# Attention and feed-forward kernel: one order of work at the turns of half batches, and a batch's scores for both halves in one stretch, partly in free PSUM columns

## The chip, the cores and the metric

The kernel runs on one core of a Trainium2 chip. The metric is the device time of one execution, in microseconds (us). An execution is timed as a whole; the profile's span is the part of it between the first and the last instruction that the profiler records. The core has five engines with a queue each: PE (matmuls, with weight loads shown apart as PEld), DVE (vector), ACT (activations and copies), POOL (a second, slower vector engine) and SP, which here issues all DMA transfers in order. SBUF is the on-chip memory, PSUM the accumulators that PE writes and DVE and ACT read.

## The reference

For each of 8 batches (576 tokens, 8 heads of 64): an attention over 32 memories per head, then a gated feed-forward layer of width 512 → 2048 → 512.

```python
a   = softmax(phi, axis=2)                    # over the 576 tokens
k_m = einsum('bhsm,bhsd->bhmd', a, k);  v_m = einsum('bhsm,bhsd->bhmd', a, v)
p   = softmax(q @ k_m.T / 8, axis=-1)         # 576 x 32 per head
x   = (p @ v_m) as (4608, 512)
h   = x @ w_in
out = (h * clip(h + 3, 0, 6) / 6) @ w_out
```

All is float32. Because `p` has 32 columns per head, the kernel folds `v_m` into `w_in` once per batch ("fold", `fo`/`vh`/`vl`: the matmuls of L428 and their two halves of a number, L439 and L448) and multiplies the probabilities by the folded weights.

## The kernel before, in words

Float32 products are made from halves of numbers: a value is cast to a rounded part (**high**) and a remainder (**low**), and three matmuls (high·high, high·low, low·high) make one product.

**Stages.** Batches 0 to 2 serve to convert the weights as well. From batch `FIRST` = 3 on runs the steady stage: batches 3 to 7, each of two halves (256 and 320 tokens; of the 320 the last 64 go into a separate "rest" product). A half has 8 `Unit`s of 256 columns of the hidden layer, a unit two steps; so a batch has 32 **steps**, 0 to 15 for half 0 and 16 to 31 for half 1. At step s, in the order in which it is written (and so queued on every engine; nothing reorders it):

- `gemm1` (PE, L716): six matmuls into a bank `ph`; `relu` (ACT, L722); `gate` (DVE, L735, and in half 1 L739 for the rest).
- On odd steps the unit's sums: `sum_first` (DVE L745), `sum_second` (POOL L749, 256 columns, and L750, 128). On even steps `high(1)` (ACT L756, 128x512) and `low(1)` (DVE L761, 128x512) of the unit just summed.
- The words of the tables `EVERY`, `STEADY`, `FOURTH` for this step: a string such as `6 xa.N.0` puts the attention piece `xa.N.0` of the next batch (N; C is this batch, M the one after next) at step 6.
- On odd steps `high(0)` (ACT L756, 128x384) and `low(0)` (DVE L761, 128x384).
- `half_step(s-3)`: the unit's share of the second matmul (`products`, PE L688). The scheme takes seven products for eight: part 0 (A11, M5, M2) is nine matmuls into banks m0 and m1, part 1 (A22, M6, M7, M1) is twelve into m2 and m3, nine of them with weights that a DMA brings (`stream`, issued by `fetch_streams`, L684).

So PE does 15 or 18 matmuls a step. At the **turn** of a half (its last unit, at steps 18 and, of the next batch, 2), the four banks leave: `leave_first` and `leave_second` read them (ACT L789 to L795, DVE L798, L799), `leave_third` makes two additions of 128x512 on POOL (L803, L804) and then issues the store (SP, L806).

**Resting batches.** In batches 4 and 6, between steps 2 and 3, PE runs 96 matmuls for the rest columns of two batches (`rest_stage`, `RestUnit`, L822 to L829); the words of steps 0 to 2 are played within it.

**The attention words** that matter here: `fetch` loads folded-weight inputs (L217, 512 KB, a ring of two buffers); `xa` subtracts the maximum from phi (DVE L309, 128x512, and L306, 64x128 twice), `xe` is its exponential (ACT L313); `mem` (PE L323), `nr`/`nk`, `tp`/`tk` make the memories; `sc` is the scores (PE L361, 32x256 or 32x320 tiles, into the one buffer `psc`), `ct` their transposition (DVE L377); `cm` the maxima (DVE L387), `cs` their subtraction (POOL L391), `ex` the exponential (ACT L394), `ds` and `dr` sums and reciprocals (DVE L387, L398, L399), `dm` the scaling (POOL L403), `bt` the transposition back, `bh` (ACT L412) and `bl` (POOL L417) the halves of the probabilities.

Of the kernel before, what the change touches and what calls it, by code (L numbers as in the profile page):

```python
# [27 lines left out]
NG = 2  # L28
# [86 lines left out]
def attention_ffn_kernel(ctx: ExitStack, tc: tile.TileContext, pn, pt, kv, kl, qt, w1, w2, out):  # L115
# [584 lines left out]
    class Unit:  # L700
# [62 lines left out]
        def products(self, part):  # L763
# [8 lines left out]
            def stream(x):  # L772
# [4 lines left out]
                (("A22", 2, 1, kept(1)), ("M6", 3, 1, part and stream(1)), ("M7", 3, 0, part and stream(2)),  # L777
# [8 lines left out]
        def leave_first(self):  # L786
# [24 lines left out]
    sums = {}  # L811
# [144 lines left out]
    with tc.manual_schedule():  # L956
# [32 lines left out]
        UNBOUND = ("tw", "ts", "th", "to2", "rp", "fs")  # L989
# [49 lines left out]
        for s in range(total_steps + LAG + 1):  # L1039
# [8 lines left out]
            if s < total_steps:  # L1048
# [76 lines left out]
```

## Time and profile before

| | |
|---|---|
| median of three executions | 705.54 us (703.06, 705.54, 1340.69) |
| profiled execution, span | 705.24 us, 703.2 us |
| PE busy, share of the span | 680.7 us, 97% |
| DVE, ACT, POOL busy | 532.1, 388.1, 333.0 us |
| mean granted clock of PE | 0.998 |
| DMA traffic | 162.86 MB, mean 232 GB/s |

The page also gives the chain of work that ended last: PE 47%, DVE 27%, DMA 9%, ACT 7%, POOL 3%. The profiled execution took 705.24 us, 2.0 us more than its span. In the rows further down, the first two numbers of a timeline row are the start and the length in us, x9 says that nine alike stand together, and a bracket tells how long the engine had been idle before and what released it. On POOL and DVE a length includes time in which an instruction that has been issued waits for the other.

### The profile page before, as it was taken

What the parts mean: (1) busy time and instruction counts of PE and PEld (TensorE: products, weight loads), DVE (VectorE), ACT (ScalarE), POOL (GpSimd) and SP (SyncE); (2) the same over time, 40 slices, a digit from 0 to 9 for tenths busy, and PEclk for the clock granted to TensorE, in tenths of its full rate; (3) what the DMA queues carried; (4) which work ended last, traced back from release to release, by engine and by line L of the source; (5) the groups of instructions that cost most, each with busy time, mean ns of one, the idle gap of its engine ahead of it and who ended that gap; (6) DMA issues with size and microseconds to landing.
All of it is one profiled execution on the core that took longest, in us unless ns stands there. A gap on an engine that the chain in (4) does not pass through costs nothing.

```text
span 703.2 us, 14752 instructions
## 1 busy us (share of the span) xinstructions
PE 680.7 (97%) x5622; PEld 577.2 (82%) x5622; DVE 532.1 (76%) x962; ACT 388.1 (55%) x786; POOL 333.0 (47%) x333
## 2 busy tenths in 40 slices
PE   8999999999999999999999999899999999999997
PEld 3456777878877787789889998799988999889997
DVE  4899987776466455566998869977898778987765
ACT  4677785554344455554655655555465555655543
POOL 2645330396564574632545435453457334554433
PEclk9999999999999999999999999999999999999999
DMA  9988573655671784899673877749675593736351
GB/s 353 421 328 314 181 270 125 225 178 178 270 260 47 277 291 132 302 375 343 221 260 118 265 273 271 275 166 332 216 262 191 155 323 114 270 118 219 121 180 47
DMA packets 66270, 162.86 MB, mean 232 GB/s; under 512 B 6808, under 2 KB 13976, under 8 KB 63640
## 3 DMA queue, kind: packets, MB, share of 16 engines
q1 hardware_dynamic: 66120, 161.86, 65.2%
q8 instruction: 44, 0.72, 0.4%
q14 instruction: 26, 0.21, 0.1%
q10 hardware_dynamic: 80, 0.07, 0.0%
HBM read 135.68 MB, written 26.22 MB: 230 GB/s over the span
## 4 chain that ended last, share of the span: by engine, by line
PE 47%; DVE 27%; DMA 9%; ACT 7%; issue 4%; POOL 3%; SPq 2%; ACTq 0%; POOLq 0%; DVEq 0%
PE acc L688 17%; PE acc L545 11%; PE ph L491 7%; PE ph L716 7%; DVE rounded L761 7%; DVE gated L735 3%; DVE gated L745 3%; DVE both L448 2%; DMA stream<-kept 2%; DMA w<-w_kept 2%; ACT rounded L756 2%; PE pk L323 2%; DMA kvt<-in_kv 2%; PE pv L428 2%; DMA kept<-stage 1%
## 5 line engine op out<-in xcount | busy, mean ns | idle before, releaser
L688 PE MATMUL acc<-w,rounded 128*128 128x256 f32 x1248 | 177.7, 282 | 4.4 <-DVE rounded L761 3.8
L688 PEld LDWEIGHTS acc<-w,rounded 128*128 128x128 f32 x1248 | 157.7, 188 | 26.7 <-issue 10.8
L749 POOL TENSOR_TENSOR gated<-gated 128x256 f32<-128x256 f32 x80 | 76.8, 961 | 189.0 <-DVE gated L735 158.2
L761 DVE TENSOR_TENSOR rounded<-gated,rounded 128x384 fp32r<-128x384 f32 (+1 forms) x160 | 133.2, 833 | 38.0 <-ACT rounded L756 32.5
L716 PE MATMUL ph<-probs,both 128*128 128x256 f32 (+1 forms) x960 | 150.4, 292 | 0.0
L756 ACT CAST rounded<-gated 128x384 fp32r<-128x384 f32 (+1 forms) x160 | 90.6, 567 | 95.3 <-DVE gated L745 89.2
L716 PEld LDWEIGHTS ph<-probs,both 128*128 128x128 f32 x960 | 131.6, 188 | 0.2
L722 ACT ACTIVATE gf<-ph,three 128x256 f32<-128x256 f32 (+1 forms) x160 | 79.9, 499 | 42.3 <-PE ph L716 40.7
L545 PE MATMUL acc<-w,ghi 128*128 128x512 f32 x384 | 101.0, 398 | 0.1
L688 PE MATMUL acc<-stream,rounded 128*128 128x256 f32 x720 | 97.3, 279 | 1.5 <-DMA stream<-kept 1.3
L688 PEld LDWEIGHTS acc<-stream,rounded 128*128 128x128 f32 x720 | 88.6, 188 | 3.6 <-DMA stream<-kept 2.5
L545 PEld LDWEIGHTS acc<-w,ghi 128*128 128x128 f32 x384 | 68.9, 188 | 23.9 <-issue 5.7
L735 DVE SCALAR_TENSOR_TENSOR gated<-gf,ph 128x256 f32<-128x256 f32 x160 | 65.5, 410 | 27.0 <-ACT gf L722 26.9
L491 PEld LDWEIGHTS ph<-probs,both 128*128 128x128 f32 x528 | 75.0, 188 | 11.2 <-DVE gf L507 5.2
L491 PE MATMUL ph<-probs,both 128*128 128x256 f32 (+1 forms) x528 | 78.5, 297 | 2.7 <-DVE gf L507 2.6
L507 DVE SCALAR_TENSOR_TENSOR gf<-gf,ph 128x576 f32<-128x576 f32 x44 | 33.0, 750 | 40.8 <-ACT gf L501 40.6
L501 ACT ACTIVATE gf<-ph,three 128x576 f32<-128x576 f32 (+2 forms) x52 | 36.5, 703 | 43.0 <-PE ph L491 38.1
L545 PE MATMUL acc<-w,glo 128*128 128x512 f32 x192 | 54.0, 390 | 0.0
L448 DVE TENSOR_TENSOR both<-pv,both 128x512 fp32r<-128x512 f32 x62 | 42.3, 682 | 14.9 <-ACT both L439 14.7
L525 DVE TENSOR_TENSOR glo<-gf,ghi 128x512 fp32r<-128x512 f32 x44 | 39.1, 892 | 12.8 <-PE acc L545 7.0
L439 ACT CAST both<-pv 128x512 fp32r<-128x512 f32 x62 | 36.1, 584 | 20.7 <-DVE both L448 13.6
L194 POOL TENSOR_TENSOR w<-tmp,raw 128x512 uint32<-128x512 uint32 x14 | 21.8, 1580 | 45.2 <-DVE tmp L184 24.5
(106 smaller groups left out, 886.9 us busy)
## 6 DMA issues: line engine op xcount, KB each, us to landing
stream<-kept SPq DMA_DIRECT2D x186, 256.0 KB, 4.4
kvt<-in_kv SPq DMA_DIRECT2D x32, 516.0 KB, 7.0
w<-w_kept SPq DMA_DIRECT2D x32, 512.0 KB, 6.0
raw<-in_w SPq DMA_DIRECT2D x16, 512.0 KB, 8.6
raw<-in_w SPq DMA_DIRECT2D x8, 1024.0 KB, 7.9
out_t<-o SPq DMA_DIRECT2D x16, 512.0 KB, 3.3
w<-w_kept SPq DMA_DIRECT2D x8, 1024.0 KB, 7.8
kept<-stage SPq DMA_DIRECT2D x24, 256.0 KB, 4.4
```

The costliest lines, as they stand in the source:

```text
L448: nc.vector.tensor_tensor(both[:, 1], src, both[:, 0].bitcast(F32), ALU.subtract)
L491: nc.tensor.matmul(dst, w[:, g, fs], x[:, g * n : (g + 1) * n], start=(i == 0), stop=(i == len(seq) - 1),)
L501: nc.scalar.activation(self.gf, self.h, AF.Relu, bias=three)
L525: nc.vector.tensor_tensor(self.glo[:, :n], self.gated(), self.ghi[:, :n].bitcast(F32), ALU.subtract)
L545: nc.tensor.matmul(accs[self.b, self.rest, k].rearrange("p (x c) -> p x c", c=VC), left[:, t * P : (t + 1) * P], w, start=k in self.first ...
L688: nc.tensor.matmul(dst, left[l], right[r], start=begin and n == 0, stop=end and n == 2, skip_group_check=True)
L716: nc.tensor.matmul(h, w[:, g, fs], x[:, g * self.n : (g + 1) * self.n], start=(i == 0), stop=(i == len(seq) - 1))
L722: nc.scalar.activation(self.gf, self.h[k], AF.Relu, bias=three)
L735: nc.vector.scalar_tensor_tensor(dst, by_tile(self.gf), 6.0, by_tile(self.h[k]), ALU.min, ALU.mult)
L749: nc.gpsimd.tensor_tensor(g[:, 2:4], g[:, 0::8], g[:, 1:8:6], ALU.subtract)
L756: nc.scalar.copy(self.parts[0][:, at], self.g[:, 1:8][:, at])
L761: nc.vector.tensor_tensor(low[:, at], self.g[:, 1:8][:, at], high[:, at].bitcast(F32), ALU.subtract)
```

## The change

1. The scores of both halves are made at step 14, behind that step's products (the word `later` divides the words of a step): half 0's into columns 256 to 511 of bank `ph0` and into the first 256 columns of the running half's bank m1, half 1's into `psc`; the transpositions follow (those of half 0 one per bank). Before, half 0's stood at step 16 and half 1's at step 20. The other attention words move with them, most to one step earlier.
2. The loads `fetch.N.0` and `fetch.N.1` move from steps 5 to 11 to steps 0 to 2, `fetch.N.3.1` from step 29 to 27; some of the words `vh`, `vl`, `bh.C.1`, `bl.C.1` move to one or two steps later.
3. In part 1 of the products M6 and M7 (bank m3) come first, then A22 and M1 (bank m2); `leave_second` reads m3 first.
4. `leave_third` becomes `leave_fourth`, `leave_fifth` and `store`: one addition behind the sums of each of the next two odd steps, the store behind that. In resting batches all three stay together at the first turn.

```diff
 STEADY = """
-0 fo.C.3 vh.C.3.0 vl.C.3.0 / 3 vh.C.3.1 / 4 vl.C.3.1 bh.C.1 / 5 bl.C.1
+0 fetch.N.0.0 fo.C.3 vh.C.3.0 / 1 fetch.N.0.1 vl.C.3.0 fetch.N.1.0 / 2 fetch.N.1.1 / 4 vh.C.3.1 / 5 vl.C.3.1 / 6 bh.C.1 / 7 bl.C.1
 """
 EVERY = """
-0 sp.N / 5 fetch.N.0.0 / 6 xa.N.0 / 7 xe.N.0 fetch.N.0.1 / 8 xa.N.1 xa.N.2 / 9 xe.N.1 fetch.N.1.0 / 10 xe.N.2 / 11 mem.N fetch.N.1.1
-/ 12 nr.N nk.N q.N.0 / 13 q.N.1 / 14 tp.N tk.N / 16 sc.N.0 ct.N.0 pt.M / 17 kv.M.0
-/ 20 sc.N.1 ct.N.1 pn.M / 21 cm.N.0 cs.N.0 cm.N.1 kv.M.1 / 22 fo.N.0 vh.N.0.0 vl.N.0.0 / 23 fetch.N.2.0 vh.N.0.1 vl.N.0.1 ex.N.0 cs.N.1 fetch.N.2.1
-/ 24 ds.N.0 dr.N.0 dm.N.0 mx.M.0 / 25 fo.N.1 vh.N.1.0 vl.N.1.0 ex.N.1 / 26 vh.N.1.1 vl.N.1.1 mx.M.1 fetch.N.3.0
-/ 27 ds.N.1 dr.N.1 bt.N.0 dm.N.1 mt.M mo.M kv.M.2 / 28 fo.N.2 vh.N.2.0 vl.N.2.0 bh.N.0 / 29 vh.N.2.1 vl.N.2.1 bl.N.0 fetch.N.3.1
-/ 30 bt.N.1 kv.M.3 / 31 kv.M.4
+0 sp.N / 5 xa.N.0 / 6 xe.N.0 / 7 xa.N.1 xa.N.2 / 8 xe.N.1 / 9 xe.N.2 / 10 mem.N
+/ 11 nr.N nk.N q.N.0 / 12 q.N.1 / 13 tp.N tk.N / 14 later sc.N.0 sc.N.1 ct.N.0 ct.N.1 / 15 pt.M / 16 cm.N.0 cs.N.0 pn.M / 17 kv.M.0
+/ 20 cm.N.1 cs.N.1 ex.N.0 kv.M.1 / 21 ds.N.0 dr.N.0 dm.N.0 / 22 fo.N.0 vh.N.0.0 vl.N.0.0 / 23 fetch.N.2.0 vh.N.0.1 vl.N.0.1 fetch.N.2.1
+/ 24 mx.M.0 ex.N.1 / 25 fo.N.1 vh.N.1.0 vl.N.1.0 bt.N.0 / 26 ds.N.1 vh.N.1.1 vl.N.1.1 fetch.N.3.0
+/ 27 dr.N.1 dm.N.1 mx.M.1 fetch.N.3.1 / 28 fo.N.2 vh.N.2.0 vl.N.2.0 bh.N.0 kv.M.2 / 29 mt.M vh.N.2.1 vl.N.2.1 bl.N.0 mo.M
+/ 30 kv.M.3 / 31 bt.N.1 kv.M.4
 """
...
+        def beside(self, hf):
+            return self.b > FIRST and hf == 0
...
+                if self.beside(hf):
+                    self.psc[hf] = [ph[0][:, W[0] :], sums[self.b - 1, 0][1][:, :VC]]
...
-                (("A22", 2, 1, kept(1)), ("M6", 3, 1, part and stream(1)), ("M7", 3, 0, part and stream(2)),
+                (("M6", 3, 1, part and stream(1)), ("M7", 3, 0, part and stream(2)), ("A22", 2, 1, kept(1)),
                  ("M1", 2, 0, part and stream(0))),
...
-            nc.vector.scalar_tensor_tensor(o[:, 0::3], m1, 1.0 / 6.0, x[:, 0::3], ALU.mult, ALU.subtract)
-            nc.vector.scalar_tensor_tensor(o[:, 0::3], m67, 1.0 / 6.0, o[:, 0::3], ALU.mult, ALU.add)
+            nc.vector.scalar_tensor_tensor(o[:, 0::3], m67, 1.0 / 6.0, x[:, 0:2], ALU.mult, ALU.subtract)
+            nc.vector.scalar_tensor_tensor(o[:, 0::3], m1, 1.0 / 6.0, o[:, 0::3], ALU.mult, ALU.add)
...
                 if k:
                     unit.sum_first()
                     unit.sum_second()
+                    if len(leaving) > 1:
+                        leaving.pop(0)()
...
+                for w in said[:soon]:
                         play(group(w))
...
             unit = half_step(s - LAG - 1, ...)
+            if s < total_steps:
+                for w in said[soon + 1 :]:
+                    play(group(w))
+            if not s % 2 and len(leaving) == 1:
+                leaving.pop()()
```

How the order of instructions moves at three places follows. In the changed kernel a line of the units has a number that is higher by 8 (L761 is now L769, L745 is L753, L749 and L750 are L757 and L758); of the attention by 2 to 8.

**First place: DVE at steps 5 to 8 of batches 4 to 7**, from the gate of step 5 on. `rounded<-gated` is a low part, `pnat<-pnat,nmxb` is `xa`, `both<-pv` is `vl.C.3.1`, `gated<-gated` is `sum_first`. Before:

```order
L735 SCALAR_TENSOR_TENSOR gated<-gf,ph_2966 128x256
L745 TENSOR_TENSOR gated<-gated 128x256
L761 TENSOR_TENSOR rounded<-gated,rounded 128x384
L735 SCALAR_TENSOR_TENSOR gated<-gf,ph_2965 128x256
L761 TENSOR_TENSOR rounded<-gated,rounded 128x512
L309 TENSOR_TENSOR pnat<-pnat,nmxb 128x512
L735 SCALAR_TENSOR_TENSOR gated<-gf,ph_2966 128x256
L745 TENSOR_TENSOR gated<-gated 128x256
L761 TENSOR_TENSOR rounded<-gated,rounded 128x384
L735 SCALAR_TENSOR_TENSOR gated<-gf,ph_2965 128x256
L761 TENSOR_TENSOR rounded<-gated,rounded 128x512
L309 TENSOR_TENSOR pnat<-pnat,nmxb 128x512
```

Now:

```order
L743 SCALAR_TENSOR_TENSOR gated<-gf,ph_2966 128x256
L753 TENSOR_TENSOR gated<-gated 128x256
L456 TENSOR_TENSOR both<-pv,both 128x512
L311 TENSOR_TENSOR pnat<-pnat,nmxb 128x512
L769 TENSOR_TENSOR rounded<-gated,rounded 128x384
L743 SCALAR_TENSOR_TENSOR gated<-gf,ph_2965 128x256
L769 TENSOR_TENSOR rounded<-gated,rounded 128x512
L743 SCALAR_TENSOR_TENSOR gated<-gf,ph_2966 128x256
L753 TENSOR_TENSOR gated<-gated 128x256
L311 TENSOR_TENSOR pnat<-pnat,nmxb 128x512
L308 TENSOR_TENSOR pnat<-pnat,nmxb 64x128 x2
L769 TENSOR_TENSOR rounded<-gated,rounded 128x384
```

`xa.N.0` (128x512) now stands between step 5's `sum_first` and its low part, and `xa.N.1`, `xa.N.2` between those of step 7; before, they stood behind the low parts of steps 6 and 8.

POOL at steps 5 and 7 (two sums each, and `bl.C.1` with `probs<-pT,probs`), before:

```order
L749 TENSOR_TENSOR gated<-gated 128x256
L750 TENSOR_TENSOR gated<-gated 128x128
L417 TENSOR_TENSOR probs<-pT,probs 128x640
L749 TENSOR_TENSOR gated<-gated 128x256
L750 TENSOR_TENSOR gated<-gated 128x128
```

and now:

```order
L757 TENSOR_TENSOR gated<-gated 128x256
L758 TENSOR_TENSOR gated<-gated 128x128
L757 TENSOR_TENSOR gated<-gated 128x256
L758 TENSOR_TENSOR gated<-gated 128x128
L425 TENSOR_TENSOR probs<-pT,probs 128x640
```

`bl.C.1` moves from behind step 5's sums to behind step 7's.

**Second place: POOL from the turn at step 18 on**, before (`o<-o` are the two additions, `st<-st,mx` is `cs`):

```order
L803 TENSOR_TENSOR o<-o 128x512
L804 TENSOR_TENSOR o<-o 128x2x256
L749 TENSOR_TENSOR gated<-gated 128x256
L750 TENSOR_TENSOR gated<-gated 128x128
L749 TENSOR_TENSOR gated<-gated 128x256
L750 TENSOR_TENSOR gated<-gated 128x128
L391 TENSOR_TENSOR st<-st,mx 128x512
```

and now, from step 19's sums on:

```order
L757 TENSOR_TENSOR gated<-gated 128x256
L758 TENSOR_TENSOR gated<-gated 128x128
L811 TENSOR_TENSOR o<-o 128x512
L399 TENSOR_TENSOR st<-st,mx 128x640
L757 TENSOR_TENSOR gated<-gated 128x256
L758 TENSOR_TENSOR gated<-gated 128x128
L815 TENSOR_TENSOR o<-o 128x2x256
L411 TENSOR_TENSOR st<-st,sm 128x512
```

Between the sums of steps 19 and 21 stand now one addition and `cs.N.1`, and behind those of step 21 the other addition and `dm.N.0`. DVE at steps 20 and 21 (gates, `sum_first`, `mx<-st` and `sm<-st` are reductions of `cm` and `ds`), before:

```order
L761 TENSOR_TENSOR rounded<-gated,rounded 128x512
L377 STREAM_TRANSPOSE st<-psc 128x640
L735 SCALAR_TENSOR_TENSOR gated<-gf,ph_2966 128x256
L739 SCALAR_TENSOR_TENSOR rest<-gf,ph_2966 128x64
L745 TENSOR_TENSOR gated<-gated 128x256
L387 TENSOR_REDUCE mx<-st 128x16
L387 TENSOR_REDUCE mx<-st 128x20
L761 TENSOR_TENSOR rounded<-gated,rounded 128x384
```

and now:

```order
L769 TENSOR_TENSOR rounded<-gated,rounded 128x512
L395 TENSOR_REDUCE mx<-st 128x20
L743 SCALAR_TENSOR_TENSOR gated<-gf,ph_2966 128x256
L747 SCALAR_TENSOR_TENSOR rest<-gf,ph_2966 128x64
L753 TENSOR_TENSOR gated<-gated 128x256
L395 TENSOR_REDUCE sm<-st 128x16
L406 TENSOR_SCALAR sm<-sm 128x16
L407 RECIPROCAL sm<-sm 128x16
L769 TENSOR_TENSOR rounded<-gated,rounded 128x384
```

The transposition of step 20 is gone from here, `cm.N.1` stands in its place, and step 21 has the sums and reciprocals of `ds.N.0`, `dr.N.0`.

**Third place: PE at the scores.** Before, step 16 (half 1's eight tiles stood the same way at step 20):

```order
L716 MATMUL ph_2965<-probs,both 128x320 x6
L361 MATMUL psc<-qh,kvT 32x256 x8
L688 MATMUL acc<-w_6_1556,rounded 128x256 x3
L688 MATMUL acc<-stream,rounded 128x256 x9
L716 MATMUL ph_2966<-probs,both 128x320 x6
```

and now, from the products of step 14 on:

```order
L696 MATMUL acc<-stream,rounded 128x256 x3
L368 MATMUL ph_2965<-qh,kvT 32x256
L368 MATMUL acc<-qh,kvT 32x256
L368 MATMUL ph_2965<-qh,kvT 32x256
L368 MATMUL acc<-qh,kvT 32x256
L368 MATMUL ph_2965<-qh,kvT 32x256
L368 MATMUL acc<-qh,kvT 32x256
L368 MATMUL ph_2965<-qh,kvT 32x256
L368 MATMUL acc<-qh,kvT 32x256
L368 MATMUL psc<-qh,kvT 32x320 x8
L724 MATMUL ph_2966<-probs,both 128x256 x6
L696 MATMUL acc<-w_6_1556,rounded 128x256 x9
```

Sixteen tiles stand together, those of half 0 in turn in `ph_2965` (bank `ph0`) and `acc` (bank m1); two blocks of matmuls (`gemm1` into `ph1` and nine products, of which the last three write m1) stand between them and the next `gemm1` into `ph0`.

## Rows read from the trace of the kernel before

**Rows 1.** Waits view, PE: engine, what, releaser: us in total, times, longest.

```profile
PE acc L688 <- DVE rounded L761: 3.8, 11, 0.4
```

**Rows 2.** Timeline of PE, batch 4, half 0: start, length, instruction, count, idle before.

```profile
391.36 0.84 PE L716 MATMUL ph<-probs,both 128*128 128x256 f32 x6
...
393.40 0.84 PE L716 MATMUL ph<-probs,both 128*128 128x256 f32 x6
...
397.82 1.55 PE L688 MATMUL acc<-w,rounded 128*128 128x256 f32 x9
```

**Rows 3.** Timeline of PE, batch 4, half 1: steps 16 and 20 with their scores.

```profile
413.23 1.03 PE L716 MATMUL ph<-probs,both 128*128 128x320 f32 x6
...
416.26 1.04 PE L716 MATMUL ph<-probs,both 128*128 128x320 f32 x6
...
422.29 1.03 PE L716 MATMUL ph<-probs,both 128*128 128x320 f32 x6
...
425.43 1.04 PE L716 MATMUL ph<-probs,both 128*128 128x320 f32 x6
```

**Rows 4.** Timeline of PE: waits for a low part and for loads.

```profile
446.51 0.39 PE L688 MATMUL acc<-w,rounded 128*128 128x256 f32 x2
447.19 1.09 PE L688 MATMUL acc<-w,rounded 128*128 128x256 f32 x7 [0.29 <-DVE rounded L761]
...
454.72 1.09 PE L428 MATMUL pv<-w,kvT 64*32 64x512 f32 x16 [1.64 <-DMA w<-w_kept]
...
535.68 1.87 PE L688 MATMUL acc<-stream,rounded 128*128 128x256 f32 x9 [0.58 <-DMA stream<-kept]
```

**Rows 5.** Timeline of DVE, batch 4, steps 4 to 8.

```profile
389.89 0.69 DVE L761 TENSOR_TENSOR rounded<-gated,rounded 128x512 fp32r<-128x512 f32 x1
...
393.69 1.71 DVE L761 TENSOR_TENSOR rounded<-gated,rounded 128x512 fp32r<-128x512 f32 x1
...
396.37 0.42 DVE L745 TENSOR_TENSOR gated<-gated 128x256 f32<-128x256 f32 x1
397.38 0.85 DVE L761 TENSOR_TENSOR rounded<-gated,rounded 128x384 fp32r<-128x384 f32 x1 [0.58 <-ACT rounded L756]
...
399.71 0.57 DVE L306 TENSOR_TENSOR pnat<-pnat,nmxb 64x128 f32<-64x128 f32 x2
```

**Rows 6.** Timeline of POOL, batch 4, steps 5 to 7.

```profile
392.55 0.46 POOL L750 TENSOR_TENSOR gated<-gated 128x128 f32<-128x128 f32 x1
392.97 1.89 POOL L417 TENSOR_TENSOR probs<-pT,probs 128x640 fp32r<-128x640 f32 x1
396.48 0.92 POOL L749 TENSOR_TENSOR gated<-gated 128x256 f32<-128x256 f32 x1 [1.63 <-DVE gated L735]
```

**Rows 7.** Timeline of ACT, batch 4, steps 6 and 7.

```profile
393.04 0.62 ACT L756 CAST rounded<-gated 128x512 fp32r<-128x512 f32 x1
394.34 0.48 ACT L722 ACTIVATE gf<-ph,three 128x256 f32<-128x256 f32 x1 [0.68 <-PE ph L716]
```

**Rows 8.** Timeline of DVE, the rest stage of batch 4.

```profile
378.64 1.37 DVE L829 TENSOR_TENSOR rounded<-total,rounded 128x128 fp32r<-128x128 f32 x1
```

**Rows 9.** Timeline of POOL, same place.

```profile
378.40 1.47 POOL L804 TENSOR_TENSOR o<-o 128x512 f32<-128x512 f32 x1
```

**Rows 10.** Timeline of DVE, batch 4, steps 20 and 21.

```profile
427.20 0.84 DVE L377 STREAM_TRANSPOSE st<-psc 128x640 f32<-128x640 f32 x1
...
428.73 1.40 DVE L387 TENSOR_REDUCE mx<-st 128x16 f32<-128x512 f32 x2
430.05 1.20 DVE L761 TENSOR_TENSOR rounded<-gated,rounded 128x384 fp32r<-128x384 f32 x1
```

**Rows 11.** Timeline of PE, batch 4, step 23: the products that read that low part.

```profile
431.67 1.18 PE L688 MATMUL acc<-w,rounded 128*128 128x256 f32 x9
```

**Rows 12.** Groups by form, POOL, whole span: busy us, mean ns, idle before.

```profile
L804 POOL TENSOR_TENSOR o<-o 128x512 f32<-128x512 f32 x10 | 13.4, 1339 | 1.7 <-DVE o L799 1.7
...
L391 POOL TENSOR_TENSOR st<-st,mx 128x640 f32<-128x640 f32 x8 | 12.5, 1565 | 2.0 <-DVE mx L387 2.0
```

More of the change, by code (lines that the diff above doesn't have):

```diff
@@ L250, in load_q @@
         loaded.setdefault(b, {})["q", hf] = heads
-    vw, probs = {}, {}
+    vw, probs, sums = {}, {}, {}
     class Attention:
@@ L349, in turned @@
             nc.scalar.copy(self.kvT, self.pq[:, :, :P])
+        def beside(self, hf):
+            return self.b > FIRST and hf == 0
         def scores(self, hf):
             if (self.b, hf) == (0, 1):
-                self.psc = [bank(W[hf]) for _ in range(NG)]
+                self.psc[hf] = [bank(W[hf]) for _ in range(NG)]
             else:
-                psc = self.psum("psc")
-                self.psc = [psc[:, g, : W[hf]] for g in range(NG)]
-                self.psc_whole = psc[:, :, : W[hf]]
+                if self.beside(hf):
+                    self.psc[hf] = [ph[0][:, W[0] :], sums[self.b - 1, 0][1][:, :VC]]
+                else:
+                    self.psc_whole[hf] = self.psum("psc")[:, :, : W[hf]]
+                    self.psc[hf] = [self.psc_whole[hf][:, g] for g in range(NG)]
             for j in range(NJ):
@@ L361, in scores @@
                     nc.tensor.matmul(
-                        self.psc[g][j * M : (j + 1) * M],
+                        self.psc[hf][g][j * M : (j + 1) * M],
                         self.kvT[rows, g, j * M : (j + 1) * M],
                         loaded[self.b]["q", hf][j][rows, :],
-                        start=True,
+                        start=not (self.beside(hf) and g),
                         stop=True,
                         tile_position=(g * D, j * M),
+                        skip_group_check=self.beside(hf),
                     )
@@ L372, in scores_turn @@
             st = st.rearrange("p (g s) -> p g s", g=NG)
-            if (self.b, hf) == (0, 1):
-                for g in range(NG):
-                    nc.vector.transpose(st[:, g], self.psc[g])
+            if (self.b, hf) == (0, 1) or self.beside(hf):
+                for g in (1, 0):
+                    nc.vector.transpose(st[:, g], self.psc[hf][g])
             else:
-                nc.vector.transpose(st, self.psc_whole)
+                nc.vector.transpose(st, self.psc_whole[hf])
         def by_token(self, hf):
@@ L809, in leave_third @@
             )
-    sums = {}
     class RestUnit:
@@ L987, in rows_of @@
             return {k: [w for w in ws if w.split(".")[0] in UNBOUND or int(w.split(".")[1]) < B] for k, ws in rows.items()}
-        UNBOUND = ("tw", "ts", "th", "to2", "rp", "fs")
+        UNBOUND = ("later", "tw", "ts", "th", "to2", "rp", "fs")
         n = starts[5]
@@ L1055, in attention_ffn_kernel @@
                     unit.sum_second()
+                    if len(leaving) > 1:
+                        leaving.pop(0)()
                 elif s >= 2 and not (resting and i == 2):
                     finish_unit(units[s // 2 - 1], 1)
+                said = rows.get(i, ())
+                soon = said.index("later") if "later" in said else len(said)
                 if not resting:
-                    for w in rows.get(i, ()):
+                    for w in said[:soon]:
                         play(group(w))
```

19 lines of the change are left out of this document (13 added, 6 removed).

## The prediction

> **What bounds the kernel now.** I read the page's share of busy time first: PE is busy 97% of the span, so what counts is whether PE gets longer work or waits. The waits view of PE then says for what it waits in the steady stage: eleven times for a low part from DVE, 3.8 us in all [rows 1], and the timeline has single waits for loads [rows 4]. Third comes the pace of PE: an even step of half 0 takes 393.40 − 391.36 = 2.04 us [rows 2], 18 matmuls at 0.113; in half 1 the six matmuls of L716 take 1.03 instead of 0.84 [rows 2, 3], so 2.04 + 0.19 = 2.23. Everything longer is an excursion or a wait. Last come DVE and POOL, for the low parts hang on them: a DVE instruction with two SBUF inputs stands still while POOL works. L761 with 512 columns, issued at 393.69, took 1.71 us, with POOL's L417 from 392.97 to 394.86 [rows 5, 6]: it ended 0.54 behind POOL's end. POOL also gets in between two DVE instructions that stand next to each other: its addition, issued at 378.40, ran ahead of DVE's small L829 of 378.64, which took 1.37 [rows 8, 9]. So what the change does to POOL's place in the order matters as much as what it does on PE.
>
> **The parts, against the profiled 705.24 us** (span 703.2 and 2.0 around it; the median of the runs shown, 705.54, is 0.3 above).
>
> *Waits for low parts that go.* An average wait shows 3.8/11 = 0.35 us of idle time [rows 1], but costs more: the nine matmuls from 446.51 on run to 448.28, so 1.77 instead of 1.18 [rows 4, 11], 0.59 where 0.29 is shown. With 0.29 or 0.30 on top that is 0.64 each. Eight of the eleven stand where the change moves the cause: three at step 29 (sums and transposition of step 27 now stand at 25 and 26), two at step 1, two at step 5 of the batches without a rest stage (two additions at once at the turn), one at step 21 of batch 7. About one of them returns, in halves, at steps 5 and 7, for the two additions still come there. 7 × 0.64 = **−4.5** (bounds 0 and 8 × 0.64 = −5.1).
>
> *Loads.* One `fo` waited 1.64 for its input [rows 4]; that load is issued two steps, some 4 us, earlier: **−1.64**. The products at 535.68 took 1.87 instead of 1.18 and had been idle 0.58 before [rows 4, 11]: 1.27, with a 512 KB load ahead of their streams that now goes earlier: **−1.27** (bound 0 each). The four loads put into steps 0 to 2 are 2 MB ahead of later streams on SP; in those steps no stream is due, so they cost nothing; if that cover is gone, one such wait a batch returns.
>
> *The joint excursion.* Step 16 took 416.26 − 413.23 = 3.03, so the scores of half 0 cost 0.80; step 20 took 3.14, so 0.91 [rows 3]. The 64 columns more cost 0.11, so 256 cost 0.44, and 0.36 is left that one excursion costs as such. Joined, it is paid once: −0.36. Against it stands that the scores must find step 14's `gate` done, since they write beside what it reads; they come 1.4 us behind `gemm1`, against relu and gate of the same step, and I put the wait at 0.3. Four batches have scores to make (4 to 7, in batches 3 to 6): 4 × −0.06 = **−0.2**. The trace has no such wait; the bounds are −0.91 each (all of one excursion) and +0.5.
>
> *Order of the products, slots, split of the additions as such*: as many instructions of the same shapes; 0. What the split moves is place 2.
>
> *Place 1: steps 5 to 9 of batches 4, 5 and 6* (batch 7 has no next batch, and in batch 3 other words stand there). `xa` now stands ahead of the low part instead of behind it. At step 5 it takes POOL's turn: L750 (0.46, at 392.55 [rows 6]) comes 0.5 later, so L756 starts at 393.5 instead of 393.04, and ACT has `bh` (640 columns, about 0.7) and the exponential of `xa.N.0` (512 columns, about the 0.62 of L756 [rows 7]) ahead of relu 7, which starts at 395.2 instead of 394.34 [rows 7]; `sum_first` of step 7 then starts at 396.1 (0.48 of relu [rows 7], and a gate of as many columns as L745 has, 0.42 [rows 5]), a little ahead of its 396.37 of now, because L309 no longer stands before it [rows 5]. From there DVE and POOL take turns: L749 (0.92 [rows 6]) to 397.2; L309 to 397.7 (POOL's end + 0.54, as above); L750 to 398.0; the first L306 to 398.2 (0.57 for two [rows 5]); `bl` on POOL, which took 1.89 with a wait of some 0.3 in it [rows 6], to 399.6; the second L306 to 399.8; and only now the low part, 0.45 more: 400.2. It ended at 397.38 + 0.85 = 398.23 [rows 5], and PE, which took 1.55 for these nine matmuls instead of 1.18 [rows 2, 11], was already waiting for it. So all of 400.2 − 398.2 ≈ 1.95 falls on PE: 3 × 1.95 = **+5.85** (bounds: 0, if `bl` comes behind the low part; 3 × 2.4, if every handover costs 0.15 more).
>
> *Place 2: steps 19 to 23 of batches 3 to 6.* POOL now has an addition behind step 19's sums, `cs.N.1` behind step 20, an addition behind step 21's sums. The first delays step 20's low part, but that has a margin: today L377 begins behind it at 427.20 [rows 10], and `cm.N.1`, about half of 1.40 [rows 10], takes the place of that 0.84, so DVE is free at about 427.9. Then `cs.N.1` runs on POOL, a mean of 1.57 [rows 12], some 1.3 without its own waits, to 429.2, and `sum_first` of step 21 ends 0.27 behind it (half of 0.54, for half the columns): 429.5. POOL's two sums end at 430.5 (0.92 + 0.46 [rows 6], less overlap), and the second addition (mean 1.34 [rows 12], 1.28 without waits) at 431.7. The low part of step 21, which stands behind the short `ds` and `dr`, ends 0.41 behind that (0.54 × 384/512): 432.15, instead of 430.05 + 1.20 = 431.25 [rows 10]. PE reads it with the third of the nine matmuls that begin at 431.67, at 431.90 [rows 11]; without step 20's excursion 0.91 earlier, at 430.99. The wait is 432.15 − 430.99 ≈ 1.2: 4 × 1.2 = **+4.8** (bounds 0, if the addition comes behind the low part, and 4 × 1.6, with the means of rows 12).
>
> The Trainium skill speaks against the shorter handovers used here: its page "SBUF — State Buffer", section "SBUF: two separate sides", calls the port pair of DVE and POOL an exclusive lock that is held for the whole instruction, while the other fully blocks. The blocking agrees with rows 5 and 6; the end at +0.54, where the same instruction takes 0.69 beside an idle POOL [rows 5], does not show a whole instruction behind POOL's end. By the page each of some three handovers at seven places would cost 0.15 more, an estimate of +3.2, and the sum would be about 711.5.
>
> *Sum.* −4.5 − 1.64 − 1.27 − 0.2 + 5.85 + 4.8 = +3.05, so 705.24 + 3.05 = **708.3 us**.
>
> **The rivals.** *A, as summed*: 708.3. *B, one of the two places does not bite* (DVE gets its low part in ahead of POOL): 708.3 − 5.85 = 702.4 or 708.3 − 4.8 = 703.5. For it: margins of 0.3 to 0.5 decide who is first at both. Against: POOL's instruction is queued ahead at each. *C, neither bites*: 705.24 − 7.6 = 697.6. Against it: DVE's 1.71 and 1.20 for low parts [rows 5, 10] show that one POOL instruction suffices. *D, the waits for low parts do not go but move on* (the change does not do what it says): 708.3 + 4.5 = 712.8. For it: POOL has as many additions as before, and each still falls beside some low part. *E, PE waits for the transpositions of the shared banks*: the order puts `gemm1` of step 16 and the last three matmuls of the next part 0 behind DVE's reading of `ph0` and m1; between lie eight tiles, one `gemm1` and six products, some 2.1 us at the pace of rows 2, and the DVE must do 0.84 us [rows 10] and what is queued ahead of it. If it is late by 0.7 each, +2.8: 711.1. The Trainium skill's page "PSUM — Partial Sum Buffer", section "PSUM bank collisions raise a hardware error", has the rule behind this: two engines are to be kept apart by bank, not by address, so the columns are free and the bank is not. No run shown here has such a wait. *F, slower*: the split additions each block a low part that PE needs at once. There are 10 turns with two; 2 are in resting batches, and place 2 holds 4, so 20 − 4 = 16 at most; a blocked low part costs 1.34 − 0.5 of margin = 0.84: +13.4, 721.7. It decides if the margin of low parts (read three steps after their gate) is under half an us everywhere; against it, rows 1 has eleven waits in 160 steps, with POOL 47% busy.
>
> **How the numbers follow.** Chances: A 0.42, B 0.22, C 0.10, D 0.10, E 0.06, F 0.10. The time is A's. The range goes from C's upper part and B's lower bounds, 699.5, to D with its own errors, 714.5; outside are F and most of C, 0.18. A measurement of this kernel tells 2%, 14.1 us, from no change: faster is below 691.1, which only C with the largest gain of the excursion (697.6 − 3.4) comes near: 0.02. Slower is above 719.3: most of F, 0.08. The rest, 0.90, is the same.
>
> **What the profile after would show.** Right: a wait of PE for a low part at step 9 of batches 4 to 6, about 2 us each with what rows 2 shows now, and one at step 23 of batches 3 to 6 of some 1.2; none at steps 29 and 1; no wait for `w` and one excursion of about 1.4 to 1.7 at step 14. In the timeline of DVE, L306 and the low part behind it long, beside `bl` on POOL. Wrong: PE waits at other steps, or for DVE's transpositions (E); the low parts of steps 7 and 21 short, ahead of POOL's instruction (B, C); many low parts of over 1 us behind the additions (F).

## The result, and the profile after

The changed kernel took **713.71 us** (median; 711.16 to 714.75), the one before 705.57 in the same comparison: ratio 1.0115, 95% interval 1.0088 to 1.0141, so slower by about 8 us, inside the 2% that count as no change. One execution of the kernel before took 1340.69 us, and the ratio leaves it out. The forecast was 708.3 with a range of 699.5 to 714.5.

The waits view of PE after, beside [rows 1]:

```profile
PE acc L696 <- DVE rounded L769: 12.8, 12, 2.4
...
PE ph L368 <- DMA qh<-in_qt: 2.2, 1, 2.2
...
PE acc L696 <- DMA stream<-kept: 0.8, 1, 0.8
```

There are twelve waits for low parts where there were eleven, but they come to 12.8 us instead of 3.8, and there is one of 2.2 us for `q`, which the kernel before did not have. The wait for `w` of [rows 4] is gone. To see where, I took the start of each step's first L716 (L724 after) and subtracted the pace of [rows 2, 3]: 2.04 us for an even step, 1.70 for an odd one (15 matmuls in place of 18), 0.19 more in half 1. Worked out so from both timelines, these are the main steps that differ, in us beyond the pace (a dash is 0.05 or less; step 2 of batch 3 has no products and is left out):

```
step             0    1    2     4    5    7    9    10    14   15   16   20   21   23   29
batch 3 before   3.11 1.73  -    2.38 0.73  -    -    -   0.27  -   0.80 0.91  -    -   0.58
        after    3.12 1.73  -    1.27 0.67  -   0.38 2.52 5.13 0.55  -    -   0.32 1.37  -
batch 4 before    -   0.70 12.11  -    -    -   0.37  -   0.28  -   0.80 0.91  -    -   0.58
        after     -    -   12.11  -    -    -   2.48 2.49 2.13 0.18 0.06 0.06  -   1.32  -
batch 5 before   2.94  -    -    0.29 1.13  -   0.79  -   0.28  -   0.80 0.91  -    -   0.59
        after    1.23  -    -     -   0.63 0.65 2.70 2.52 1.45 0.13  -    -   0.30 1.38  -
batch 6 before    -   0.56 13.96  -    -    -   0.37  -   0.28  -   0.80 0.91  -    -    -
        after     -    -   12.11  -    -    -   2.48 4.12 1.28 0.18 0.06 0.06  -   1.32  -
```

(`mem` costs 2.5, now at step 10, before at 11; `tp` costs 0.27, now at step 13, before at 14.) Place 1 is step 9, place 2 are steps 21 and 23, and step 14 of batch 3 stands out.

**Place 1**, batch 4. PE, the nine products of step 9:

```profile
401.94 0.39 PE L696 MATMUL acc<-w,rounded 128*128 128x256 f32 x2
404.53 1.07 PE L696 MATMUL acc<-w,rounded 128*128 128x256 f32 x7 [2.20 <-DVE rounded L769]
```

DVE, `xa` and the low part of step 7 behind it:

```profile
400.64 1.23 DVE L311 TENSOR_TENSOR pnat<-pnat,nmxb 128x512 f32<-128x512 f32 x1
401.79 2.09 DVE L308 TENSOR_TENSOR pnat<-pnat,nmxb 64x128 f32<-64x128 f32 x2
403.91 0.56 DVE L769 TENSOR_TENSOR rounded<-gated,rounded 128x384 fp32r<-128x384 f32 x1
```

and POOL beside it:

```profile
402.15 1.58 POOL L425 TENSOR_TENSOR probs<-pT,probs 128x640 fp32r<-128x640 f32 x1
```

Two L308 that took 0.57 in [rows 5] now take 2.09: `bl` (L425) got in between them, and the low part could begin only behind the second. It ends at 404.47, and PE goes on at 404.53.

**Place 2**, batch 4. DVE at steps 20 and 21 (low part, maxima, `sum_first`, low part), beside [rows 10]:

```profile
433.79 1.32 DVE L769 TENSOR_TENSOR rounded<-gated,rounded 128x512 fp32r<-128x512 f32 x1
435.04 0.80 DVE L395 TENSOR_REDUCE mx<-st 128x20 f32<-128x640 f32 x1
...
436.23 1.24 DVE L753 TENSOR_TENSOR gated<-gated 128x256 f32<-128x256 f32 x1
...
438.73 1.41 DVE L769 TENSOR_TENSOR rounded<-gated,rounded 128x384 fp32r<-128x384 f32 x1
```

POOL: the first addition, `cs.N.1`, the second addition:

```profile
432.95 1.61 POOL L811 TENSOR_TENSOR o<-o 128x512 f32<-128x512 f32 x1
...
435.93 1.27 POOL L399 TENSOR_TENSOR st<-st,mx 128x640 f32<-128x640 f32 x1 [1.36 <-DVE mx L395]
...
438.45 1.27 POOL L815 TENSOR_TENSOR o<-o 128x512 f32<-128x512 f32 x1
```

PE at step 23, beside [rows 11]:

```profile
438.77 0.39 PE L696 MATMUL acc<-w,rounded 128*128 128x256 f32 x2
440.19 1.09 PE L696 MATMUL acc<-w,rounded 128*128 128x256 f32 x7 [1.03 <-DVE rounded L769]
```

Each of the three POOL instructions holds up the DVE instruction next to it: 1.32 for 0.69, 1.24 for 0.42, 1.41 for about 0.5.

**Step 14 of batch 3.** PE, from the last products ahead of the scores to the next `gemm1` (half 0's 16 rows alternate between `ph` and `acc`; the first is shown):

```profile
326.01 0.50 PE L696 MATMUL acc<-stream,rounded 128*128 128x256 f32 x3
328.73 0.37 PE L368 MATMUL ph<-qh,kvT 64*32 64x256 f32 x1 [2.21 <-DMA qh<-in_qt]
...
329.55 2.01 PE L368 MATMUL psc<-qh,kvT 64*32 64x320 f32 x16
331.49 1.40 PE L724 MATMUL ph<-probs,both 128*128 128x256 f32 x6
```

The DMA view of 317 to 325 us (KB each, median us from issue to landing):

```profile
qh<-in_qt SPq DMA_DIRECT2D x2, 320.0 KB, 9.6
w<-w_kept SPq DMA_DIRECT2D x1, 512.0 KB, 8.1
qh<-in_qt SPq DMA_DIRECT2D x1, 512.0 KB, 8.9
```

`q` is issued at steps 11 and 12 (before: 12 and 13) and took 9 to 10 us to land, behind a `w` load and among streams. (In batch 3 the loads `fetch` do not move to steps 0 to 2: there the table `FOURTH` puts them at steps 7, 9, 11 and 16, so that the one of step 11 stands right ahead of `q`.) Half 1's was needed at step 20 in the kernel before and is needed at step 14 now, half 0's at 16 before. Behind the wait PE was slow as well: 1.40 for the six matmuls that take 0.84. The windows view (PE busy, granted clock, DMA share, GB/s) shows it:

```profile
328.70:329.00 0.30, 0.27 (x13) 1.00 1.00 386
329.10:332.40 3.30, 3.30 (x35) 0.50 0.99 363
332.50:335.00 2.50, 2.50 (x22) 1.00 0.83 264
...
570.40:571.30 0.90, 0.87 (x7) 1.00 0.00 0
571.40:574.70 3.30, 3.30 (x47) 0.50 0.00 0
574.90:578.00 3.10, 3.10 (x61) 1.00 0.18 34
```

The second group is step 10 of batch 6, behind place 1's wait of 2.20 (PE works again from 570.43): 4.12 instead of 2.49.

### The profile page after: what moved, and what is told of

Its sections match the earlier page's. It is cut to its first block, busy times and chain, and to the rows that moved or that the text cites. A ratio compares the mean times of both kernels' runs of the same rounds, so it can differ in the third digit from the quotient of the medians.

```text
span 712.0 us, 14822 instructions
## 1 busy us (share of the span) xinstructions
PE 681.1 (96%) x5618; PEld 578.8 (81%) x5622; DVE 538.3 (76%) x966; ACT 386.7 (54%) x786; POOL 337.1 (47%) x333
## 4 chain that ended last, share of the span: by engine, by line
PE 57%; DVE 17%; DMA 10%; ACT 6%; POOL 4%; issue 3%; SPq 1%; ACTq 0%; DVEq 0%; POOLq 0%
PE acc L696 22%; PE ph L724 11%; PE acc L553 9%; PE ph L499 7%; DVE rounded L769 3%; DMA stream<-kept 3%; PE pv L436 2%; PE pk L325 2%; PE acc L885 2%; DVE gated L743 2%; DVE gf L515 1%; DVE pnat L308 1%; DVE gated L753 1%; DMA kept<-stage 1%; DMA qh<-in_qt 1%
## 5 line engine op out<-in xcount | busy, mean ns | idle before, releaser
L696 PE MATMUL acc<-w,rounded 128*128 128x256 f32 x1248 | 174.9, 279 | 12.9 <-DVE rounded L769 12.8
L757 POOL TENSOR_TENSOR gated<-gated 128x256 f32<-128x256 f32 x80 | 76.9, 961 | 201.5 <-DVE gated L743 183.1
L769 DVE TENSOR_TENSOR rounded<-gated,rounded 128x384 fp32r<-128x384 f32 (+1 forms) x160 | 133.0, 832 | 30.5 <-ACT rounded L764 25.2
L724 PE MATMUL ph<-probs,both 128*128 128x256 f32 (+1 forms) x960 | 152.1, 294 | 0.0
L724 PEld LDWEIGHTS ph<-probs,both 128*128 128x128 f32 x960 | 132.7, 189 | 2.8 <-issue 2.6
L696 PE MATMUL acc<-stream,rounded 128*128 128x256 f32 x720 | 110.4, 280 | 0.8 <-DMA stream<-kept 0.8
L696 PEld LDWEIGHTS acc<-stream,rounded 128*128 128x128 f32 x720 | 95.1, 188 | 11.3 <-issue 4.2
```

The costliest lines, as they stand in the source:

```text
L696: nc.tensor.matmul(dst, left[l], right[r], start=begin and n == 0, stop=end and n == 2, skip_group_check=True)
L724: nc.tensor.matmul(h, w[:, g, fs], x[:, g * self.n : (g + 1) * self.n], start=(i == 0), stop=(i == len(seq) - 1))
L757: nc.gpsimd.tensor_tensor(g[:, 2:4], g[:, 0::8], g[:, 1:8:6], ALU.subtract)
L769: nc.vector.tensor_tensor(low[:, at], self.g[:, 1:8][:, at], high[:, at].bitcast(F32), ALU.subtract)
```

## The experiments

Each kernel is the changed one with the edit shown, unless it says otherwise; ratios are to the kernel before. Two places move the whole time even where no edit is aimed at them, so the arguments below go by single steps. Steps 14 and 15 of batch 3 hold 5.68 in the changed kernel, but 2.83, 3.54, 3.20 and 3.90 in e1, e2, e5 and e6, which leave the loads of `q` where they were and show no lower clock there. Step 4 of batch 3 holds from 1.23 (e6, e10) to 2.40 (e2, e5).

**e1: `xa` behind the low parts.**

```diff
-/ 5 xa.N.0 / ... / 7 xa.N.1 xa.N.2 /
+/ 5 later xa.N.0 / ... / 7 later xa.N.1 xa.N.2 /
```

> Changed kernel (713.7 us) with xa.N.0 and xa.N.1/xa.N.2 put behind the low parts of steps 5 and 7 on DVE; all else as it was. Theory (POOL's bl gets ahead of the low part of step 7 because L308 stands before it): the wait at step 9 of batches 4 to 6 falls from about 2.4 us to the 0.4 that the kernel before had, -2.0 each, and the stretch at the lower clock at step 10 of batch 6 (1.6) goes with it: about 706. Rival (ACT is what is late: bh and the exponential ahead of relu 7): the wait stays above 1.5 each, 712 to 714.

Measured 709.36 (1.0063, 1.0040 to 1.0086). This is between the theory and the rival: step 9 of batches 4 and 6 fell from 2.48 to 1.67 only, that of batch 5 from 2.70 to 2.03, and PE then waited for something else:

```profile
401.12 0.97 PE L724 MATMUL ph<-probs,both 128*128 128x256 f32 x6 [1.51 <-DVE gated L743]
```

DVE in the same kernel, with `bl` on POOL:

```profile
397.69 1.88 POOL L425 TENSOR_TENSOR probs<-pT,probs 128x640 fp32r<-128x640 f32 x1
398.07 2.05 DVE L311 TENSOR_TENSOR pnat<-pnat,nmxb 128x512 f32<-128x512 f32 x1
...
400.65 0.42 DVE L743 SCALAR_TENSOR_TENSOR gated<-gf,ph 128x256 f32<-128x256 f32 x1
```

Now `xa` itself stands still beside `bl` until 0.55 behind its end, and the next gate stands behind `xa`.

**e5: as e1, and `bl` two steps later.**

```diff
-... / 6 bh.C.1 / 7 bl.C.1
+... / 8 bh.C.1 / 9 bl.C.1
```

> The kernel with xa behind the low parts (709.4 us) with, besides, bh.C.1 and bl.C.1 at steps 8 and 9 instead of 6 and 7. There the wait of 1.7 at step 9 of batches 4 to 6 was PE's for the gate of step 8, which stood behind xa, which stood still beside bl. Theory (bl at step 7 next to xa is the whole of place 1, by whichever of DVE's instructions comes behind): step 9 falls to 0.2 or less, -1.6 each, and no stretch at the lower clock remains at step 10: about 704 with the wait for q still in. Rival (bl only moves the wait on, to what stands behind step 9's sums): 1.0 or more stays at steps 10 to 12, 708 to 710.

703.62 (0.9979, 0.9970 to 0.9989), as the theory had it; step 9 is 0.19 in batches 4 and 6, and 0.72 in batch 5, about what the kernel before has there (0.79). The core's row shows that PE's clock was granted in full on the whole:

```profile
core 0: 702.7 us, clock 1.000
```

So place 1 is `bl` next to `xa`, and what stands behind on DVE is late. (The edit moves `bh` on ACT as well; that `bl` is the one that counts is seen in the rows, where L308 and L311 end just behind L425.) In batch 5 a wait remains that the theory did not have: step 7 holds 1.31, where the changed kernel has 0.65, because there the second addition of the turn runs beside `xa`:

```profile
471.42 1.60 POOL L815 TENSOR_TENSOR o<-o 128x512 f32<-128x512 f32 x1
471.80 1.77 DVE L311 TENSOR_TENSOR pnat<-pnat,nmxb 128x512 f32<-128x512 f32 x1
```

**e2: both additions at the turn.**

```diff
-                    leaving.extend((unit.leave_fourth, unit.leave_fifth, unit.store))
+                    unit.leave_fourth()
+                    unit.leave_fifth()
+                    unit.store()
```

> Changed kernel with both POOL additions and the store at the turn itself, as in the kernel before; products and slots in the new order. Theory (the addition behind step 21's sums holds up the low part of step 21): the waits at steps 21 and 23, together 1.65 in each of four batches, go, -6.6, and in batches 5 and 7 some 0.6 in all returns at steps 4 to 7: about 707.5. Rival (cs.N.1 alone, behind step 20, makes the low part late): at least 0.8 stays at step 23, 710 to 711.

712.99 (1.0109, 1.0085 to 1.0134): 5.5 above the theory and 2 above the rival's upper end, so neither. Step 23 is clean, but step 21 now holds between 0.84 and 1.16, where it held between 0 and 0.32. Besides, step 5 of batches 5 and 7 holds 1.49, where it held 0.63, and step 21 of batch 7 holds 0.86, where it held nothing. The additions at the turn hold up the sums of step 19. POOL and DVE in batch 4:

```profile
429.50 1.29 POOL L815 TENSOR_TENSOR o<-o 128x512 f32<-128x512 f32 x1 [0.32 <-DVE o L807]
429.79 1.27 DVE L753 TENSOR_TENSOR gated<-gated 128x256 f32<-128x256 f32 x1
```

The kernel before has the same delay at the same place, and there step 20's excursion covered it:

```profile
423.52 1.26 DVE L745 TENSOR_TENSOR gated<-gated 128x256 f32<-128x256 f32 x1
```

**e6: the first addition at the turn, the second behind the next odd step's sums.**

```diff
-                    leaving.extend((unit.leave_fourth, unit.leave_fifth, unit.store))
+                    unit.leave_fourth()
+                    leaving.extend((unit.leave_fifth, unit.store))
```

> Changed kernel (713.7 us) with the first POOL addition at the turn (it reads only what ACT has written) and the second behind the next odd step's sums, where the first stood; nothing of the two behind step 21's sums any more. Theory (that second addition holds up step 21's low part): 1.37 at step 23 falls to 0.5 or less and nothing is added at step 21, -0.9 to -1.4 in each of four batches, about 709. Rival (dm.N.0 or cs.N.1 holds it up as well): step 23 keeps 1 us or more, 713.

708.82 (1.0047, 1.0029 to 1.0064). Step 23, which held 1.32 to 1.38, now holds 0.43 to 0.47; step 21 holds about 0.32 in all four batches, which in batches 4 and 6 is 0.3 more than in the changed kernel. The low part of step 21 in this kernel takes its free time:

```profile
434.40 0.49 DVE L769 TENSOR_TENSOR rounded<-gated,rounded 128x384 fp32r<-128x384 f32 x1
```

**e3: `q` at step 10, batch 3's `fetch.N.1.0` two steps later.**

```diff
-/ 7 fetch.N.0.0 / 9 fetch.N.0.1 / 11 fetch.N.1.0 / 16 fetch.N.1.1
+/ 7 fetch.N.0.0 / 9 fetch.N.0.1 / 13 fetch.N.1.0 / 16 fetch.N.1.1
...
-/ 10 mem.N / 11 nr.N nk.N q.N.0 / 12 q.N.1 / 13
+/ 10 mem.N q.N.0 q.N.1 / 11 nr.N nk.N / 13
```

> Changed kernel with the loads q.N.0 and q.N.1 issued at step 10, right behind mem, instead of at steps 11 and 12, and batch 3's fetch.N.1.0 at step 13 instead of 11. Theory (the joint scores need both halves of q two steps after their issue, where half 1's had eight): step 14 falls from 5.7 to 1.6 in batch 3 and from 2.3 to 1.6 in batch 4, -4.8, and PE's clock stays at full speed there: about 709. Rival (the DMA engines are full in that stretch, 397 GB/s, so the wait only moves to the streams): batch 3 keeps over 3 us of it, 712 to 714.

711.14 (1.0077, 1.0048 to 1.0106). Step 14 is 1.28 in all four batches, so all waits for `q` are gone; yet only 2.6 of the 4.8 us came. In this profiled run step 4 of batch 3 held 2.33 instead of 1.27, and place 1's wait was followed by a slow stretch in batch 4 too (in batch 3 there was none any more). PE there:

```profile
401.10 1.81 PE L696 MATMUL acc<-w,rounded 128*128 128x256 f32 x7 [2.20 <-DVE rounded L769]
402.71 1.48 PE L724 MATMUL ph<-probs,both 128*128 128x256 f32 x6
```

and its windows:

```profile
401.20:404.50 3.30, 3.30 (x21) 0.50 0.00 0
406.00:409.00 3.00, 3.00 (x49) 1.00 0.96 319
```

**e4: the edits of e1, e2 and e3 together.**

> Changed kernel with the three edits together (xa behind the low parts, additions at the turn, q loads at step 10). If the three causes are independent, the gains add: 713.7 - 7.6 - 6.0 - 4.8 = about 695.3. Rival (behind each wait stands another that was covered): 700 or more.

706.19 (1.0006, 0.9984 to 1.0027): the rival. Behind the cured places stood the gate of e1 (1.67 and more at step 9) and the sums of e2 (0.88 to 1.18 at step 21, 1.49 at step 5 of batches 5 and 7).

**e7: e3, and half 1's scores made again at step 20.**

```diff
-/ 20 cm.N.1 cs.N.1 ...
+/ 20 sc.N.1 cm.N.1 cs.N.1 ...
```

> The kernel with the early loads of q (711.1 us), in which half 1's scores are made a second time at step 20, into the same bank with the same values, so that PE has again the excursion of some 0.9 us there; nothing reads the second ones. Theory (DVE and POOL set the pace of steps 19 to 23, so the excursion saved at step 20 was given back as waits): the waits at steps 21 and 23, 0.3 and 1.36, fall by about the 0.9 that step 20 gains, the time stays within 1 us, 710 to 712. Rival (the waits come from the additions alone and stand whatever PE does): the waits stay, +0.9 in each of four batches, 714.7.

710.63 (1.0073, 1.0046 to 1.0099): 0.9 us more work for PE in each of four batches, and no more time than e3, as the theory had it. PE at steps 20 and 23 of batch 4:

```profile
427.43 0.77 PE L368 MATMUL psc<-qh,kvT 64*32 64x320 f32 x16
...
435.84 0.39 PE L696 MATMUL acc<-w,rounded 128*128 128x256 f32 x2
436.71 1.07 PE L696 MATMUL acc<-w,rounded 128*128 128x256 f32 x7 [0.49 <-DVE rounded L769]
```

Step 20 gained 0.91; step 21, which held 0.3 in e3, holds nothing, and step 23 holds 0.54 to 0.81 where it held 1.36 to 1.38. So the excursion saved at step 20 had been given back as waits.

**e8: all cures**: the edits of e5, e3 and e6, and

```diff
-/ 21 ds.N.0 dr.N.0 dm.N.0 / 22 fo.N.0
+/ 22 ds.N.0 dr.N.0 dm.N.0 fo.N.0
```

> Changed kernel with xa behind the low parts, bl.C.1 at step 9, q's loads at step 10, the first addition at the turn and the second behind the next odd step's sums, and ds, dr and dm of half 0 at step 22 instead of 21. The kernel with the first three kinds of edit took 706.2; against it steps 9 to 10 should lose another 1.5 in batches 4 to 6 with 1.7 for one stretch at the lower clock, step 21 0.8 in four batches, step 5 of batches 5 and 7 0.8: about 695. Rival (each cured place uncovers the next): 702 or more.

**696.30** (0.9872, 0.9856 to 0.9889), 9 us faster than the kernel before and 1.3 above the theory. Its waits view:

```profile
PE acc L696 <- DVE rounded L769: 1.6, 4, 0.5
```

**e9: the kernel before, with the loads alone at their new steps** (shown in part; the loads are gone from steps 5 to 11, and batch 3 has them at steps 7, 9, 11 and 16).

```diff
-0 fo.C.3 vh.C.3.0 vl.C.3.0 / 3 vh.C.3.1
+0 fetch.N.0.0 fo.C.3 vh.C.3.0 vl.C.3.0 / 1 fetch.N.0.1 fetch.N.1.0 / 2 fetch.N.1.1 / 3 vh.C.3.1
...
-/ 27 ds.N.1 dr.N.1 bt.N.0 dm.N.1 mt.M mo.M kv.M.2
+/ 27 fetch.N.3.1 ds.N.1 dr.N.1 bt.N.0 dm.N.1 mt.M mo.M kv.M.2
-/ 28 fo.N.2 vh.N.2.0 vl.N.2.0 bh.N.0 / 29 vh.N.2.1 vl.N.2.1 bl.N.0 fetch.N.3.1
+/ 28 fo.N.2 vh.N.2.0 vl.N.2.0 bh.N.0 / 29 vh.N.2.1 vl.N.2.1 bl.N.0
```

> Kernel before (705.5 us) with part 2 of the change alone: the loads fetch.N.0 and fetch.N.1 at steps 0 to 2 (in batch 3 at 7, 9, 11 and 16), fetch.N.3.1 at step 27. Theory (the waits for w at 454.72 and for a stream at 535.68 in the kernel before are these loads' doing): step 0 of batch 5 falls by 1.7, step 2 of batch 6 by 1.85, nothing is added: about 702.3. Rival (2 MB ahead of the streams at the turn makes another stream late): one such wait returns per batch, 704 to 709.

701.22 (0.9936, 0.9922 to 0.9950), as the theory had it. Step 0 of batch 5 fell from 2.94 to 1.26, step 2 of batch 6 from 13.96 to 12.11, and no wait for a load came in their place. The rows that answer to those of [rows 4] show no idle time before them:

```profile
452.82 1.09 PE L429 MATMUL pv<-w,kvT 64*32 64x512 f32 x16
...
533.04 1.18 PE L689 MATMUL acc<-stream,rounded 128*128 128x256 f32 x9
```

**e10: the kernel before, with the new order of the products, of the reading and the slots alone** (part 3 of the change as its diff has it).

```diff
-                (("A22", 2, 1, kept(1)), ("M6", 3, 1, part and stream(1)), ("M7", 3, 0, part and stream(2)),
+                (("M6", 3, 1, part and stream(1)), ("M7", 3, 0, part and stream(2)), ("A22", 2, 1, kept(1)),
...
```

> Kernel before with part 3 of the change alone: M6 and M7 ahead of A22 and M1, leave_second reading bank m3 first, the slots to match; both additions at the turn. Theory (as many instructions of the same shapes; the order decides nothing by itself): within 1 us of 705.5. Rival (the nine products with streamed weights stand three matmuls earlier, and waits for streams or for DVE's low parts grow by up to 0.34 each): 707 to 710.

705.15 (0.9996, 0.9984 to 1.0009): no change, as the theory had it.

**e11: e8 with half 1's scores and transposition back at step 20.**

```diff
-/ 14 later sc.N.0 sc.N.1 ct.N.0 ct.N.1 / ... / 20 cm.N.1
+/ 14 later sc.N.0 ct.N.0 / ... / 20 sc.N.1 ct.N.1 cm.N.1
```

> The kernel with all the cures (696.3 us) with half 1's scores and transposition back at step 20, so two excursions again; half 0's stay at step 14 in the free columns. Theory (joining saves 0.31 of PE a batch, but the waits at steps 21 and 23, 0.32 and 0.14, exist only since step 20 has no excursion, so joining is worth next to nothing): 695.5 to 697.5. Rival (joining pays in full, and DVE's transposition of 0.84 at step 20 delays the sums behind it): 0.31 x 4 and a new wait of 0.5 or more in each batch, 699 or more.

698.75 (0.9905, 0.9890 to 0.9920): between the two, and 1.2 above the theory's upper end. In batch 4, steps 14, 15, 20, 21 and 23 hold 0.74 + 0.14 + 0.91 + 0 + 0.39 = 2.18 with two excursions, 1.28 + 0.13 + 0 + 0.32 + 0.14 = 1.87 joined: about 0.3 a batch, 1.3 in all, is what joining brings at these steps once the rest is cured. Of the theory, the 0.32 at step 21 went with the second excursion, but step 23 held 0.26 more. The two ratios differ by 0.0033, 2.3 us, and with both intervals taken together (root of the sum of squares) by 0.8 to 3.9; the spans of the two profiled runs differ by 0.6 only (step 4 of batch 3 held 0.4 more in e8).

## Why the prediction was right, and where it was not

*Waits for low parts* (−4.5): −5.4 from the table and batch 7 (step 29 −1.8, step 1 −1.3, steps 4 to 8 of batches 5 and 7 −1.5, step 21 of batch 7 −0.8). Right, with the halves that return at steps 5 and 7.

*Loads* (−1.64, −1.27): −1.7 and −1.85, and e9, which moves the loads alone, shows both. The second was under-sized: I took only the wait between two rows, while the step as a whole shows 13.96 − 12.11. That the 2 MB early cost nothing is right too.

*Joint excursion* (−0.2): where `q` is there, steps 14 and 15 hold about 1.41 against 0.80 + 0.91, −0.3 in each of four batches, −1.2. The wait for step 14's gate that I put against it is not to be seen.

*Place 1* (+5.85): 2.11 + 1.91 + 2.11 = +6.1, by the mechanism and order given, L308 by L308. e1 and e5, with their rows, show that `bl` is the cause and that the low part was only the nearest victim.

*Place 2* (+4.8): steps 21 and 23 together +6.0. e6 shows 0.9 of the 1.4 at step 23 to be the second addition's, e7 that a 0.9 longer step 20 hides as much: both halves of the working. The 0.3 at step 21 of two batches was missing. As the order shows, the gate of step 19 stands behind DVE's reading of the banks at the turn; that step 20's excursion had covered it fits e7 and e11, where step 21 holds nothing, but no run moves that reading.

These terms give −5.4 − 1.7 − 1.85 − 1.2 + 6.1 + 6.0 = +2, where I had +3 (the sum as written makes 3.04, not 3.05, which leaves 708.3). The other 6.8 of the 8.8 us by which the spans differ (712.0 to 703.2) comes from steps that the prediction passed over. **Of the moved words it costed the loads of `w`, not those of `q`**: the wait at step 14 is 5.68 − 1.41 = 4.3 in batch 3, 0.9 in batch 4, 0.2 in batch 5, +5.3 with the slow clock in batch 3; e3 removes it. Without the slow clock behind it, the same wait of batch 3 came to 1.4 to 2.5 in e1, e2, e5 and e6. The lower clock at step 10 of batch 6 is +1.6; that a wait of PE can be followed by a lower clock stood in no term. The remainder of −0.1 is made of parts of both signs, the largest −1.1 at step 4 of batch 3, a step that varies as much among the other runs. So the mechanism was right for the terms summed, but the step that failed was to take the moved loads of `q` as free. The time fell near the range's upper end, by a mechanism that none of the rivals had: that it lies inside the range at all, by 0.8 us, is luck, for that end was set by rival D, which did not come.

The rivals: B, C and F did not come. (F's price was too high besides: of 20 additions, four in resting batches and four of place 2 leave 12 and not 16, so 718.4.) D did not: the waits named at steps 29 and 1 and at step 21 of batch 7 are gone in the changed kernel. E did not: the waits view after has, for this stage, no row in which PE waits for a transposition of the shared banks. The rule of the Trainium skill's page "PSUM — Partial Sum Buffer", section "PSUM bank collisions raise a hardware error", thus cost nothing here; that it would without the six products between, no run shows. On the handover the rows after agree with those before: L769 of 433.79 ends at 435.11, 0.55 behind the end of POOL's L811 at 434.56, and L753 ends 0.27 behind that of L399. The lock of which the Trainium skill's page "SBUF — State Buffer", section "SBUF: two separate sides", speaks agrees with these rows; the reading of it that the prediction priced at +3.2, a whole instruction behind the other's end, does not (the two take 0.69 and 0.42 undisturbed).

## What to carry to other kernels

Where work is taken off the bound engine at a step, look which late instruction of other engines that step had been covering: here 0.9 us of matmuls saved at step 20 came back as waits until instructions of POOL were moved as well. A joined stretch needs all its inputs at the earlier of the two times, so the load of every operand, not only of those that the change names, is to be followed back to its issue. When DVE and POOL block each other, moving the victim uncovers the next one; move the long POOL instruction to where no input of the bound engine stands behind it.

## What the runs showed that I had not expected

Behind some waits of PE of about 2 us, its clock fell from 1.00 to 0.50, the lower of its two levels (1.2 of 2.4 GHz), while PE was at work again, and was back at 1.00 behind the stretch (the windows under step 14). It did not follow each such wait: in the changed kernel it came behind place 1 of batch 6 (a wait of 2.20), not of batch 4 (2.20) or batch 5 (2.40); in e3 behind those of batches 4 and 6, not 5; in e1 behind a wait of 1.84 in batch 5, where step 10 held 4.29. The six runs of the changed kernel go with it at their ends: the mean granted clock was 0.997 in the run of 711.16 us and 0.992 in that of 714.75, and 0.005 × 712 = 3.6 is their difference; but 713.62 came at 0.992 as well. In the profiled runs of e5 and e8, which have no wait of that length in this stage, it was 1.000. What decides whether a wait is followed by a slow stretch stays open.

In batches 4 and 6 of the changed kernel the nine products of an odd step took 1.23 instead of 1.18 from step 15 to 21 (0.06 a step in the table) at a granted clock of 1.00; in e5 and e6 they did not. The kernel before has the same from step 22 of batch 7 on, so it does not come from the change. I have no cause for it.
